# One order of work items per place in a group: four lists instead of one

## The chip, the cores and the metric

The kernel runs on one NeuronCore of one Trainium2 chip. The metric is device time in microseconds, the median of the runs shown. The engines are TensorE (PE, with its weight loads PEld), VectorE (DVE), ScalarE (ACT), GpSimd (POOL) and SyncE (SP, which here issues DMAs).

## The reference

Two branches of the same input x (2048 tokens, 640 wide) are mixed by a gate per token.

```python
def _A_ref(x, mem0, Wq, Wk, Wv, Wo, seg_len):      # 32 heads of 192, seg_len 32, M = 8 memory rows
    ...
    for s in range(n_seg):                          # 64 segments
        xs = x[:, s * seg_len:(s + 1) * seg_len, :].copy()
        h = jnp.concatenate([mem, xs], axis=1)      # 40 rows
        q, k, v = ...                               # h times Wq, Wk, Wv
        scores = jnp.einsum('bhqe,bhke->bhqk', q, k) * scale
        scores = jnp.where(mask[None, None], scores, -1000000000.0)
        p = _softmax(scores, axis=-1)
        o = jnp.einsum('bhqk,bhke->bhqe', p, v)
        o = jnp.einsum('bhte,hed->btd', o, Wo)
        mem = o[:, :M, :].copy()                    # memory of the next segment
        outs.append(o[:, M:, :])
    ...
g = _sigmoid((x * gate_w).sum(-1, keepdims=True))
return g * a + (1 - g) * b                          # b: a gated GELU feed-forward of x
```

The eight memory rows of a segment come out of the segment before it, so the 64 segments form a chain.

## The kernel before

The feed-forward branch and the gate come first (about 177 us). Then `segment(s)` is called for s = 0 to 63. Four segments form a group; a segment's place in its group is q = s % 4.

The rows that go through the chain are 32: the 8 memory rows and the first 24 rows of the segment's own. The other 8 own rows ("left" rows) do not feed the memory of their own segment; their Q, K and V are computed for four segments at once, in 32 rows, ahead of time.

The 32 heads are handled in four octets of eight heads. Even segments go through octets 0, 1, 2, 3, odd ones through 3, 2, 1, 0; i below counts in the order of use. `PROG` is the hand-written order of a segment's items, and the order of each engine's instructions follows from it. All engines work their own queue in that order, and SP issues its DMAs in that order too. The items:

- `("g", n, k)`: projections, contraction slice k of 5, of the matrices in `GROUPS[n]`. n = 0 is Q and K of octet 0; 1 is V 0, Q 1, K 1; 2 is V 1, Q 2; 3 is K 2; 4 is V 2, Q 3; 5 is K 3; 6 is V 3. Each matrix takes four 384-wide matmuls (L1039, or L226 where the loaded rows are kept). In place 0 the V of the left rows goes along from octet 1 on. After k = 4 ACT copies the results out of PSUM (L1059 for Q and K, L1062 for V).
- `tq`, `tk`: DVE transposes Q or K (L1073). `sc`: mask and scores on PE (L1080, L1088, L1093), then maximum and subtraction on DVE (L1107, L1109). `ex`: exponential on ACT (L1119), sum, reciprocal and two products on DVE (L1121 to L1126).
- `pt`: p is transposed on PE (L1139, L1144) and copied by ACT (L1157; for the last octet L1151 and DVE's L1153). `pv`: p times V on PE (L1172, L1174), copied into `uT` by ACT (L1183; a part of the last octet by DVE, L1188).
- `("wo", i, h)`: two pairs of heads of octet i times their rows of Wo, L1201 for octets 0 to 2, L1224 for the last. After `wo 2 1` ACT and DVE add the four partial sums (`half_sums`, L1207, L1210). In place 3 `wo` also multiplies the left rows (L1201 again).
- `("lf", q, u, k)`: in place q, Q and K of the left rows of a later group, unit u, slice k (L882 and L226). `("le", q, u, m)`: their copy (ACT, L887) and transpose (DVE, L889); for m = 1 also a store to HBM on SP's queue (L893). An `le` that stands behind the last `wo` is put off until Z and the transposed memory are done. `("vb", k)`: in place 3, V of the left rows for the next group (L1012). Items for another place are skipped.

At the end of a segment DVE adds up Z (L1340) and transposes the memory rows (L1344, `Tm`), and the next segment's first Q waits for that.

Most weights stay in SBUF. Seventeen pieces do not fit twice: octet 0's and octet 3's slices of Q, K and V (14 of 15) share slots, and three pieces of Wo share slots with three others. `swap_loads` is called after each item: a piece that has just been used is replaced by its partner (L597), which is wanted at the end of the same segment. So each segment loads 14 pieces of 384 KB and three of 480 KB, issued by SP in the order of use: K's slice 0, Q, K, V, Wo. Behind them in SP's queue stand the load of left Q and K for the next segment (`stg_load`, issued at `sc 3`, L942), the loads of the other branch's result (L947, L951), and the stores (L893, L951, L956).

PSUM banks for projections, `lf` and `pv` come from `misc_bank`, the least recently taken of those that are free in the list's order.

Of the kernel before, what the change touches and what calls it, by code (L numbers as in the profile page):

```python
# [231 lines left out]
def _build(nc, A_x, A_mem0, A_Wq, A_Wk, A_Wv, A_Wo, seg_len, w_gate, w_up, w_down,  # L232
# [9 lines left out]
    KT = Dm // 128  # L242
# [3 lines left out]
    NOCT = NT // 4  # L246
# [251 lines left out]
    def piece_view(key, o):  # L498
        if key[0] == 3:
# [1 line left out]
        return bview(o, GQ)  # L501

    GROUPS = [[(0, 0), (1, 0)], [(2, 0), (0, 1), (1, 1)], [(2, 1), (0, 2)], [(1, 2)], [(2, 2), (0, 3)], [(1, 3)], [(2, 3)]]
    PROG = [("g", 0, 0), ("g", 0, 1), ("g", 0, 2), ("g", 0, 3), ("g", 0, 4), ("g", 1, 0), ("g", 1, 1), ("tq", 0),
# [13 lines left out]
    assert NOCT == 4  # L518
    WOP = 4
    NWP = NT  # L520
# [4 lines left out]
    def octet(s, i):  # L525
        return i if s % 2 == 0 else NOCT - 1 - i
# [4 lines left out]

    def seg_order(s):
        keys = []
        for item in PROG:
            if item[0] == "g":
                keys += [(m, octet(s, i), item[2]) for m, i in GROUPS[item[1]]]
            elif item[0] == "wo":
                keys += [(3, p) for p in wo_pairs(s, item)]
        return keys

    orders = [seg_order(0), seg_order(1)]
    assert len(orders[0]) == len(set(orders[0])) == 3 * KT * NOCT + NWP
    partner = {}
    for m, k in [(m, k) for m in range(3) for k in range(KT)][3 * KT - NSQ:]:
# [53 lines left out]
               dma_sem="slot%d" % slot_id[key], name="%s %s" % (name, key))  # L598

    def piece(seg, key):  # L600
        order = orders[seg % 2]
        oi = last_req.get(seg, -1) + 1
        assert order[oi] == key, "pieces must be consumed in order"
        last_req[seg] = oi
        if seg == 0 and key in tmp_off:
            return left_piece(key)
        done_keys.append(key)
        return piece_view(key, res_off[key]), r_res[key]
# [15 lines left out]
    def left_piece(key):  # L624
        if key in tmp_off:
            return piece_view(key, tmp_off[key]), r_tmp[key]
        return piece_view(key, res_off[key]), r_res[key]
# [616 lines left out]
                                      pa == p_first and c == 0, pb == p_last and c == 2),  # L1244
                       reads=[ra, rb, r_uTl[pa // 4]], writes=[r_ps[LB]], name="Wol s%d p%d" % (s, pa))

    assert PROG.index(("g", [n for n, ms in enumerate(GROUPS) if (2, 1) in ms][0], KT - 1)) < PROG.index(("wo", 0, 0))
    late_at = ("g", 1, KT - 1)
    items = [item for item in PROG if item[0] not in ("lf", "le", "vb")]
    n_wo = PROG.index(items[-1])  # L1250
    rowl = [bview(wsB_off["rowl"], 768) for b in range(2)]
    r_rowl = [sreg(wsB_off["rowl"], 768) for b in range(2)]
    nqkv = [i for i, item in enumerate(PROG) if item[0] == "g"][-1]

    def left_evac(s, u, m):
        left_rows(*unit(s, u), m, lb[u, m], lst[3], r_lst[3], rowl[m], r_rowl[m])
# [7 lines left out]

    def segment(s):
        g, q = s // 4, s % 4
        held = []
        post = []
        for n, item in enumerate(PROG):
            kind, i = item[0], item[1]  # L1270
            if kind == "g":
                if n == 0:
                    left_fill(s, octet(s, 0))
                    if s:
                        S_.add("pool", lambda e: e.memset(pl_sb[0:104, :, M * ((q + 3) % 4):M * ((q + 3) % 4) + M], 0.0),
                               writes=[r_p], name="pl zero s%d" % s)
                proj(s, item)
                ki = [j for m, j in GROUPS[i] if m == 1 and item[2] == KT - 1]
                kind, i = ("k", ki[0]) if ki else ("", 0)
                if kind == "k" and i == 1:  # L1280
                    if s > 0:
                        out_store(s - 1)
                    if s + 1 < NSEG:
                        x_load(s + 1)
            elif kind == "tq":
                row_transp(s, 0, i)
            elif kind == "tk":
                row_transp(s, 1, i)
            elif kind == "sc":
                scores(s, i)  # L1290
                if i == 0 and q == 0 and g > 0:
                    left_sums(g - 1)
            elif kind == "ex":
                softmax(s, i)
            elif kind == "pt":
                p_transp(s, i)
            elif kind == "pv":
                pv_oct(s, i)
            elif kind == "lf":
                if i == q and unit(s, item[2]):  # L1300
                    if item[3] == 0:
                        for m in range(2):
                            lb[item[2], m] = misc_bank(s)
                    for m in range(2):
                        LBK[m] = lb[item[2], m]
                    left_mm(*unit(s, item[2]), item[3], unit_piece)
            elif kind == "vb":
                if q == 3 and g + 1 < NG:
                    if i == 0:
                        lb["v"] = misc_bank(s)  # L1310
                    vl_mm(s + 1, i)
            elif kind == "le":
                if i == q and unit(s, item[2]):
                    if n > n_wo:
                        post.append(item[2:])
                    else:
                        left_evac(s, *item[2:])
            else:
                held = wo_part(s, item)
                if i == 2 and item[2] == 0 and q == 0 and g > 0:  # L1320
                    outl_store(g - 1)
                if q == 3 and item != items[-1]:
                    wo_left(s, held)
            swap_loads(s, item)
            if s == 0 and item == ("g", 0, KT - 1):
# [114 lines left out]
```

## Time and profile before

| | |
|---|---|
| time, median of 3 runs | 1790.21 us (1785.28 to 1790.6) |
| span of the profiled execution, first to last instruction | 1783.4 us |
| mean granted TensorE clock | 0.998 |
| PE busy | 1629.5 us, 91% |
| DVE, ACT, POOL busy | 54%, 45%, 18% |
| moved by DMA | 524.33 MB, mean 294 GB/s |
| start of the first segment, of the last | 176.9 us, 1752.2 us |

For the profiled execution the page gives the span only; its own time is not listed apart from the three runs. A row of the timeline has the start, the length, the engine, the line, the operation, what it writes and reads with shapes, how many were merged, and in brackets the idle time before and who ended it. A row of the waits has the waiting engine and line, who was waited for, the sum in us, how often, and the longest.

### The profile page before, as it was taken

How to read it: one execution, taken by the hardware profiler on the slowest of the kernel's cores; microseconds unless marked ns; L12 is line 12 of the kernel's file. 1: busy time of each engine (PE TensorE's matmuls, PEld its weight loads, DVE VectorE, ACT ScalarE, POOL GpSimd, SP SyncE). 2: the span in 40 equal slices, each digit the busy share in tenths (PEclk: the TensorE clock that was granted, in tenths of full speed). 3: DMA queues.
4: the chain of work that ended last, by engine and by line, in shares of the span. 5: the costliest groups of instructions: out<-in, count | busy, mean ns of one | idle time of the engine just before them, and what ended most of it. 6: DMA issues, size and time to landing. Idle time of an engine off the chain costs nothing.

```text
span 1783.4 us, 80070 instructions
## 1 busy us (share of the span) xinstructions
PE 1629.5 (91%) x39162; PEld 817.9 (46%) x31501; DVE 957.7 (54%) x2932; ACT 793.8 (45%) x1835; POOL 319.8 (18%) x1099
## 2 busy tenths in 40 slices
PE   9999989899998999899899999899999989899987
PEld 4554444454444444454444444454444444454443
DVE  2223555555555655555565655555555655555554
ACT  3222444444444444444444444444444544444443
POOL 1100111111211111111111111111211111111211
PEclk9999999999999999999999999999999999999999
DMA  9815887888788887888788887888888887888786
GB/s 332 297 45 177 329 318 266 324 322 316 289 295 298 318 311 261 318 318 315 287 299 299 311 319 263 322 310 319 298 299 300 317 290 269 321 313 321 289 303 260
DMA packets 263390, 524.33 MB, mean 294 GB/s; under 512 B 97384, under 2 KB 116224, under 8 KB 263040
## 3 DMA queue, kind: packets, MB, share of 16 engines
q1 hardware_dynamic: 259912, 516.11, 79.5%
q8 instruction: 276, 4.52, 1.0%
q10 hardware_dynamic: 3128, 3.09, 0.5%
q14 instruction: 74, 0.61, 0.1%
HBM read 498.00 MB, written 21.11 MB: 291 GB/s over the span
## 4 chain that ended last, share of the span: by engine, by line
PE 69%; DMA 13%; DVE 8%; ACT 6%; issue 4%; SPq 0%; DVEq 0%; ACTq 0%
PE ps L1039 20%; PE ps L226 15%; PE ps L1201 8%; DMA arena<-in_A_Wv_dram 7%; PE ps L1172 3%; DMA left_qk_scratch<-arena 3%; PE ps L802 3%; PE ps L799 3%; PE ps L882 3%; DVE arena L889 3%; PE ps L1093 2%; PE ps L817 2%; ACT arena L887 2%; PE ps L1080 2%; PE ps L1088 2%
## 5 line engine op out<-in xcount | busy, mean ns | idle before, releaser
L1039 PE MATMUL ps<-arena 128*32 128x384 bf16 x9940 | 734.8, 328 | 58.5 <-DVE arena L1344 40.4
L226 PE MATMUL ps<-arena 128*32 128x384 bf16 x7680 | 584.4, 326 | 10.8 <-ACT arena L887 6.1
L1039 PEld LDWEIGHTS ps<-arena 128*32 128x32 bf16 x9940 | 254.0, 96 | 420.1 <-issue 244.4
L1073 DVE STREAM_TRANSPOSE arena<-arena 128x384 bf16<-128x384 bf16 x512 | 279.0, 564 | 227.0 <-ACT arena L1059 226.6
L1059 ACT ACTIVATE arena<-ps 128x384 bf16<-128x384 f32 x512 | 236.2, 489 | 176.3 <-PE ps L1039 164.4
L1201 PE MATMUL ps<-arena 128*32 128x320 bf16 x6144 | 297.0, 300 | 16.1 <-issue 15.5
L1201 PEld LDWEIGHTS ps<-arena 128*32 128x32 bf16 x6144 | 163.6, 97 | 75.7 <-issue 26.5
L1119 ACT ACTIVATE ps<-ps 104x160 f32<-104x160 f32 x256 | 74.3, 290 | 236.4 <-DVE ps L1109 236.4
L1107 DVE TENSOR_REDUCE arena<-ps 104x4 f32<-104x160 f32 x256 | 83.1, 325 | 176.0 <-PE ps L1093 175.7
L1157 ACT ACTIVATE arena<-ps 128x448 bf16<-128x448 f32 x192 | 104.8, 546 | 143.3 <-PE ps L1144 143.3
L1191 POOL COPY arena<-arena 128x96 bf16<-128x96 bf16 x256 | 68.4, 267 | 522.6 <-ACT arena L1183 419.3
L936 POOL COPY arena<-arena 128x96 bf16<-128x96 bf16 x256 | 70.0, 274 | 498.7 <-PE ps L1093 436.3
L1183 ACT ACTIVATE arena<-ps 128x480 bf16<-128x480 f32 (+1 forms) x256 | 138.1, 540 | 34.0 <-PE ps L1174 29.0
L1062 ACT ACTIVATE arena<-ps 128x384 bf16<-128x384 f32 x256 | 124.8, 488 | 52.7 <-PE ps L1039 52.4
L1172 PE MATMUL ps<-arena 128*64 128x160 bf16 x1536 | 122.1, 243 | 10.4 <-issue 3.4
L1172 PEld LDWEIGHTS ps<-arena 128*64 128x64 bf16 x1536 | 80.6, 109 | 97.9 <-ACT arena L1157 46.6
L882 PE MATMUL ps<-arena 128*32 128x384 bf16 x1280 | 111.1, 330 | 1.2 <-issue 1.2
L1174 PE MATMUL ps<-arena 128*64 128x64 bf16 x1536 | 105.1, 194 | 5.8 <-issue 5.8
L1121 DVE TENSOR_REDUCE arena<-ps 104x4 f32<-104x160 f32 x256 | 81.8, 320 | 51.6 <-ACT ps L1119 43.9
L889 DVE STREAM_TRANSPOSE arena<-arena 128x384 bf16<-128x384 bf16 x128 | 73.8, 577 | 57.4 <-ACT arena L887 52.6
L1224 PE MATMUL ps<-arena 128*32 128x160 bf16 x3072 | 77.1, 234 | 22.2 <-DMA arena<-in_A_Wo_dram 12.6
L887 ACT ACTIVATE arena<-ps 128x384 bf16<-128x384 f32 x128 | 62.4, 490 | 67.6 <-DVE arena L889 38.5
(84 smaller groups left out, 1816.7 us busy)
## 6 DMA issues: line engine op xcount, KB each, us to landing
arena<-in_A_Wk_dram SPq DMA_DIRECT2D x335, 384.0 KB, 7.7
arena<-in_A_Wv_dram SPq DMA_DIRECT2D x335, 384.0 KB, 9.4
arena<-in_A_Wq_dram SPq DMA_DIRECT2D x272, 384.0 KB, 5.6
arena<-in_A_Wo_dram SPq DMA_DIRECT2D x205, 480.0 KB, 7.4
left_qk_scratch<-arena SPq DMA_DIRECT2D x64, 192.0 KB, 2.6
arena<-left_qk_scratch SPq DMA_DIRECT2D x63, 192.0 KB, 7.8
ffn_b_scratch<-arena ACTq DMA_DIRECT2D x16, 160.0 KB, 3.7
arena<-ffn_b_scratch SPq DMA_DIRECT2D x64, 40.0 KB
```

The lines of the kernel that those rows point to most:

```text
L226: return e.add_instruction(mybir.InstMatmult(name=nm, start_tensor_calc=like["start"], stop_tensor_calc=stop, tile_size=(128, 32), tile_po ...
L882: fns.append(lambda e, outp=outp, rhs=rhs, j=j: e.matmul(outp, lhs, rhs, start=(k == 0), stop=(k == KT - 1), tile_position=(0, 32 * j)))
L889: S_.add("dve", lambda e: e.transpose(out=dst[:, :, m].rearrange("p q c i -> p c q i"), in_=rowl.rearrange("p (c r) -> p c r", r=L)), read ...
L1039: fns.append(lambda e, outp=outp, rhs=rhs, j=j: e.matmul(outp, lhs, rhs, start=(k == 0), stop=(k == KT - 1), tile_position=(0, 32 * j)))
L1059: S_.add("act", lambda e, m=m, bk=bk: e.activation(out=rows_sb[m], in_=ps[:, bk, 0:384], func=ACTF.Copy), reads=[r_ps[bk]], writes=[r_rows ...
L1062: S_.add("act", lambda e, i=i, bk=bk: e.activation(out=v_sb[i % NVB].rearrange("p (c n) -> p c n", c=3), in_=ps[:, bk, 0:384].rearrange("p ...
L1073: S_.add("dve", lambda e: e.transpose(out=dst[:, :, 0:L], in_=rows_sb[m].rearrange("p (c r) -> p c r", r=L)), reads=[r_rows[m]], writes=[r ...
L1157: S_.add("act", lambda e: e.activation(out=PT, in_=ps[:, bank, 0:PTW + 128], func=ACTF.Copy), reads=[r_ps[bank]], writes=[r_PT], name="pT ...
L1172: return [lambda e: e.matmul(full, v[:, e0:e0 + 64], PTm[:, i], start=True, stop=False, tile_position=(0, 64 * i), skip_group_check=True), ...
L1174: lambda e: e.matmul(part, vl[:, e0:e0 + 64], PTl[:, i], start=False, stop=True, tile_position=(0, 64 * i), skip_group_check=True)]
L1183: S_.add("act", lambda e: e.activation(out=apx(u[:, 0, 0, :], [[R, na], [3 * R, 4], [1, R]]), in_=ps[:, A, 0:na * W].rearrange("p (c t r) ...
L1201: fns.append(lambda e, i=i, t=t, j=j, gv=gv: e.matmul(ps[32 * j:32 * j + 32, bank, 0:2 * DJ].rearrange("p (h n) -> p h n", h=2), lhs2[i], ...
```

## The change

The single list `PROG` gives way to four lists, `PROGS[q]`, one for each place. Each holds the items that its place runs, and all are in a new order. What each item does is not touched. The bookkeeping follows: four orders of weight pieces instead of two, the last `wo` and the last `g` found in each list, and the start of a segment recognised by `("g", 0, 0)`, since the list of place 1 begins with an `lf`.

```diff
-    PROG = [("g", 0, 0), ("g", 0, 1), ("g", 0, 2), ("g", 0, 3), ("g", 0, 4), ("g", 1, 0), ("g", 1, 1), ("tq", 0),
-   ("tk", 0), ("g", 1, 2), ("sc", 0), ("ex", 0), ("g", 1, 3), ("g", 1, 4), ("tq", 1), ("g", 2, 0),
-   ("g", 2, 1), ("g", 2, 2), ("g", 2, 3), ("tk", 1), ("g", 2, 4), ("g", 3, 0), ("pt", 0), ("g", 3, 1),
-   ("sc", 1), ("tq", 2), ("lf", 1, 0, 0), ("ex", 1), ("g", 3, 2), ("g", 3, 3), ("g", 3, 4), ("lf", 1, 0, 1),
-   ("pv", 0), ("g", 4, 0), ("tk", 2), ("g", 4, 1), ("g", 4, 2), ("g", 4, 3), ("pt", 1), ("sc", 2),
-   ("lf", 1, 0, 2), ("g", 4, 4), ("pv", 1), ("g", 5, 0), ("tq", 3), ("ex", 2), ("lf", 1, 0, 3), ("g", 5, 1),
-   ("lf", 1, 0, 4), ("g", 5, 2), ("wo", 0, 0), ("le", 1, 0, 0), ("le", 1, 0, 1), ("g", 5, 3), ("wo", 0, 1),
-   ("lf", 1, 1, 0), ("lf", 0, 1, 0), ("pt", 2), ("wo", 1, 0), ("g", 5, 4), ("pv", 2), ("wo", 1, 1), ("tk", 3),
-   ("sc", 3), ("lf", 0, 1, 1), ("g", 6, 0), ("lf", 1, 1, 1), ("g", 6, 1), ("lf", 2, 1, 0), ("g", 6, 2),
-   ("ex", 3), ("g", 6, 3), ("wo", 2, 0), ("lf", 2, 1, 1), ("lf", 1, 1, 2), ("pt", 3), ("g", 6, 4),
-   ("wo", 2, 1), ("lf", 2, 1, 2), ("pv", 3), ("lf", 2, 1, 3), ("lf", 0, 1, 2), ("vb", 0), ("lf", 1, 1, 3),
-   ("vb", 1), ("lf", 1, 1, 4), ("lf", 0, 1, 3), ("lf", 0, 1, 4), ("lf", 2, 1, 4), ("vb", 2), ("le", 0, 1, 0),
-   ("le", 1, 1, 0), ("le", 1, 1, 1), ("le", 2, 1, 0), ("wo", 3, 0), ("le", 2, 1, 1), ("wo", 3, 1), ("vb", 3),
-   ("le", 0, 1, 1), ("vb", 4)]
+    PROGS = [
+        [("g", 0, 0), ("g", 0, 1), ("g", 0, 2), ("g", 0, 3), ("g", 0, 4), ("g", 1, 0), ("g", 1, 1), ("g", 1, 2),
+   ("tq", 0), ("tk", 0), ("sc", 0), ("g", 1, 3), ("ex", 0), ("g", 1, 4), ("tq", 1), ("g", 2, 0), ("tk", 1),
+   ("g", 2, 1), ("g", 2, 2), ("g", 2, 3), ("pt", 0), ("g", 2, 4), ("g", 3, 0), ("sc", 1), ("g", 3, 1),
+   ("g", 3, 2), ("g", 3, 3), ("tq", 2), ("pv", 0), ("ex", 1), ("g", 3, 4), ("g", 4, 0), ("tk", 2), ("g", 4, 1),
+   ("g", 4, 2), ("g", 4, 3), ("g", 4, 4), ("g", 5, 0), ("lf", 0, 1, 0), ("g", 5, 1), ("lf", 0, 1, 1),
+   ("sc", 2), ("g", 5, 2), ("pt", 1), ("g", 5, 3), ("tq", 3), ("lf", 0, 1, 2), ("wo", 0, 0), ("lf", 0, 1, 3),
+   ("g", 5, 4), ("tk", 3), ("ex", 2), ("lf", 0, 1, 4), ("pv", 1), ("g", 6, 0), ("g", 6, 1), ("le", 0, 1, 0),
+   ("g", 6, 2), ("pt", 2), ("sc", 3), ("g", 6, 3), ("wo", 0, 1), ("le", 0, 1, 1), ("ex", 3), ("pv", 2),
+   ("g", 6, 4), ("wo", 1, 0), ("pt", 3), ("wo", 1, 1), ("wo", 2, 0), ("pv", 3), ("wo", 2, 1), ("wo", 3, 0),
+   ("wo", 3, 1)],
+        [("lf", 1, 0, 0), ("g", 0, 0), ("g", 0, 1), ("g", 0, 2), ("g", 0, 3), ("g", 0, 4), ("lf", 1, 0, 1),
+   ("g", 1, 0), ("tk", 0), ("tq", 0), ("g", 1, 1), ("g", 1, 2), ("g", 1, 3), ("g", 1, 4), ("sc", 0),
+   ("g", 2, 0), ("lf", 1, 0, 2), ("g", 2, 1), ("tk", 1), ("ex", 0), ("g", 2, 2), ("tq", 1), ("g", 2, 3),
+   ("g", 2, 4), ("g", 3, 0), ("lf", 1, 0, 3), ("lf", 1, 0, 4), ("g", 3, 1), ("sc", 1), ("pt", 0), ("g", 3, 2),
+   ("g", 3, 3), ("g", 3, 4), ("tk", 2), ("pv", 0), ("g", 4, 0), ("g", 4, 1), ("g", 4, 2), ("tq", 2),
+   ("g", 4, 3), ("ex", 1), ("sc", 2), ("g", 4, 4), ("g", 5, 0), ("g", 5, 1), ("g", 5, 2), ("le", 1, 0, 0),
+   ("g", 5, 3), ("tq", 3), ("pt", 1), ("g", 5, 4), ("ex", 2), ("tk", 3), ("pv", 1), ("g", 6, 0),
+   ("le", 1, 0, 1), ("wo", 0, 0), ("wo", 0, 1), ("g", 6, 1), ("lf", 1, 1, 0), ("pt", 2), ("lf", 1, 1, 1),
+   ("sc", 3), ("ex", 3), ("lf", 1, 1, 2), ("pv", 2), ("lf", 1, 1, 3), ("wo", 1, 0), ("lf", 1, 1, 4),
+   ("le", 1, 1, 0), ("pt", 3), ("g", 6, 2), ("g", 6, 3), ("g", 6, 4), ("le", 1, 1, 1), ("wo", 1, 1),
+   ("wo", 2, 0), ("pv", 3), ("wo", 2, 1), ("wo", 3, 0), ("wo", 3, 1)],
+        [("g", 0, 0), ("g", 0, 1), ("g", 0, 2), ("g", 0, 3), ("g", 0, 4), ("g", 1, 0), ("tq", 0), ("g", 1, 1),
+   ("g", 1, 2), ("tk", 0), ("g", 1, 3), ("g", 1, 4), ("sc", 0), ("lf", 2, 1, 0), ("g", 2, 0), ("g", 2, 1),
+   ("g", 2, 2), ("lf", 2, 1, 1), ("tq", 1), ("g", 2, 3), ("tk", 1), ("ex", 0), ("g", 2, 4), ("sc", 1),
+   ("g", 3, 0), ("g", 3, 1), ("g", 3, 2), ("g", 3, 3), ("lf", 2, 1, 2), ("pt", 0), ("g", 3, 4), ("ex", 1),
+   ("lf", 2, 1, 3), ("pv", 0), ("g", 4, 0), ("g", 4, 1), ("lf", 2, 1, 4), ("g", 4, 2), ("g", 4, 3), ("tk", 2),
+   ("tq", 2), ("g", 4, 4), ("pt", 1), ("g", 5, 0), ("sc", 2), ("g", 5, 1), ("wo", 0, 0), ("ex", 2),
+   ("g", 5, 2), ("g", 5, 3), ("g", 5, 4), ("g", 6, 0), ("pv", 1), ("pt", 2), ("g", 6, 1), ("tq", 3), ("tk", 3),
+   ("wo", 0, 1), ("pv", 2), ("sc", 3), ("le", 2, 1, 0), ("ex", 3), ("le", 2, 1, 1), ("wo", 1, 0), ("wo", 1, 1),
+   ("g", 6, 2), ("wo", 2, 0), ("g", 6, 3), ("pt", 3), ("g", 6, 4), ("pv", 3), ("wo", 2, 1), ("wo", 3, 0),
+   ("wo", 3, 1)],
+        [("g", 0, 0), ("g", 0, 1), ("g", 0, 2), ("g", 0, 3), ("g", 0, 4), ("g", 1, 0), ("g", 1, 1), ("tq", 0),
+   ("tk", 0), ("g", 1, 2), ("sc", 0), ("g", 1, 3), ("ex", 0), ("g", 1, 4), ("g", 2, 0), ("g", 2, 1), ("tq", 1),
+   ("tk", 1), ("g", 2, 2), ("g", 2, 3), ("pt", 0), ("g", 2, 4), ("g", 3, 0), ("g", 3, 1), ("pv", 0), ("sc", 1),
+   ("tq", 2), ("g", 3, 2), ("g", 3, 3), ("g", 3, 4), ("g", 4, 0), ("wo", 0, 0), ("g", 4, 1), ("g", 4, 2),
+   ("tk", 2), ("ex", 1), ("sc", 2), ("pt", 1), ("g", 4, 3), ("g", 4, 4), ("wo", 0, 1), ("g", 5, 0),
+   ("g", 5, 1), ("ex", 2), ("g", 5, 2), ("pv", 1), ("g", 5, 3), ("g", 5, 4), ("tk", 3), ("g", 6, 0), ("tq", 3),
+   ("pt", 2), ("g", 6, 1), ("wo", 1, 0), ("g", 6, 2), ("pv", 2), ("sc", 3), ("ex", 3), ("g", 6, 3), ("vb", 0),
+   ("wo", 1, 1), ("pt", 3), ("g", 6, 4), ("wo", 2, 0), ("pv", 3), ("vb", 1), ("wo", 2, 1), ("wo", 3, 0),
+   ("wo", 3, 1), ("vb", 2), ("vb", 3), ("vb", 4)]]
...
-        for item in PROG:
+        for item in PROGS[s % 4]:
-    orders = [seg_order(0), seg_order(1)]
+    orders = [seg_order(s) for s in range(4)]
...
-        order = orders[seg % 2]
+        order = orders[seg % 4]
...
-    assert PROG.index(("g", [n for n, ms in enumerate(GROUPS) if (2, 1) in ms][0], KT - 1)) < PROG.index(("wo", 0, 0))
+    for prog in PROGS:
+        assert prog.index(("g", [n for n, ms in enumerate(GROUPS) if (2, 1) in ms][0], KT - 1)) < prog.index(("wo", 0, 0))
-    items = [item for item in PROG if item[0] not in ("lf", "le", "vb")]
-    n_wo = PROG.index(items[-1])
+    last_wo = ("wo", NOCT - 1, 1)
+    n_wos = [prog.index(last_wo) for prog in PROGS]
-    nqkv = [i for i, item in enumerate(PROG) if item[0] == "g"][-1]
+    nqkvs = [max(i for i, item in enumerate(prog) if item[0] == "g") for prog in PROGS]
...
+        n_wo, nqkv = n_wos[q], nqkvs[q]
-        for n, item in enumerate(PROG):
+        for n, item in enumerate(PROGS[q]):
-                if n == 0:
+                if item[1:] == (0, 0):
...
-                if q == 3 and item != items[-1]:
+                if q == 3 and item != last_wo:
```

## The prediction

> **What bounds the kernel now.** I read the page first, then the engine's waits for PE, then the same stretch of four segments in windows, then the timeline around each wait.
>
> ```profile
> PE 1629.5 (91%) x39162; PEld 817.9 (46%) x31501; DVE 957.7 (54%) x2932; ACT 793.8 (45%) x1835; POOL 319.8 (18%) x1099
> ...
> q1 hardware_dynamic: 259912, 516.11, 79.5%
> q8 instruction: 276, 4.52, 1.0%
> ```
>
> PE is the busy engine, but the weight queue q1 is close behind it. The windows of one group, places 0 to 3 (segments 36 to 39), show how little room each place has:
>
> ```profile
> 1079.78:1105.13 25.35, 23.59 (x615) 12.05 (x492) 15.51 (x49) 11.97 (x29) 5.42 (x18) 1.00 0.79 292
> 1105.13:1131.07 25.94, 23.42 (x593) 10.67 (x454) 15.19 (x47) 12.65 (x30) 4.55 (x16) 1.00 0.83 301
> 1131.07:1154.61 23.54, 21.25 (x553) 9.99 (x433) 13.63 (x44) 11.39 (x27) 4.49 (x16) 1.00 0.88 323
> 1154.61:1180.10 25.49, 23.66 (x628) 12.81 (x528) 12.60 (x42) 10.79 (x26) 4.49 (x16) 1.00 0.80 297
> ```
>
> Columns: length, busy PE, PEld, DVE, ACT, POOL, clock, DMA share, GB/s. Over all 16 groups the places take 25.13, 25.74, 23.91 and 25.35 us, together 100.1. Place 2 has least PE work and the busiest transfers. What PE waits for:
>
> ```profile
> PE ps L1039 <- DVE arena L1344: 40.4, 48, 1.8
> PE ps L1201 <- issue: 15.5, 23, 1.7
> PE ps L1224 <- DMA arena<-in_A_Wo_dram: 12.6, 22, 0.9
> PE ps L1039 <- DMA arena<-in_A_Wv_dram: 9.3, 19, 1.6
> PE ps L1139 <- DVE arena L1125: 7.8, 22, 0.7
> ```
>
> The first is the segment boundary (last `wo`, Z, transpose Tm, next Q): from the last 160-wide matmul group to the next Q 0.95 us pass instead of 0.07. Two are weights that have not landed. Place 2 on PE:
>
> ```profile
> 1147.75 0.34 PE L1039 MATMUL ps<-arena 128*32 128x384 bf16 x4
> 1148.49 0.35 PE L1039 MATMUL ps<-arena 128*32 128x384 bf16 x4 [0.41 <-DMA arena<-in_A_Wv_dram]
> ...
> 1152.00 0.81 PE L1224 MATMUL ps<-arena 128*32 128x160 bf16 x36
> 1153.25 0.39 PE L1224 MATMUL ps<-arena 128*32 128x160 bf16 x12 [0.44 <-DMA arena<-in_A_Wo_dram]
> 1154.61 0.35 PE L1039 MATMUL ps<-arena 128*32 128x384 bf16 x4 [0.97 <-DVE arena L1344]
> 1154.78 0.34 PE L226 MATMUL ps<-arena 128*32 128x384 bf16 x4
> ```
>
> The trace's landings explain it (means of segments 8 to 55, from the segment's first Q): in places 0, 2 and 3 the first swapped piece is issued at 0.54 and lands at 4.2 to 4.4, then one lands every 1.0 to 1.4 us: last K at 13.4, V at 14.4, 15.5, 16.5, 17.5 and 18.7, the three Wo at 19.9, 21.2 and 22.4. No order of items makes them earlier. The last Wo then needs its matmuls and the boundary, some 1.35 us, so 23.8 us is a floor for a place; place 2 stands on it. Place 1 runs 1.1 us late from the start, because a store of left rows waits at the head of SP's queue:
>
> ```profile
> 1106.33 0.38 SPq L893 DMA_DIRECT2D left_qk_scratch<-arena  x1
> ...
> 1106.76 0.50 SPq L597 DMA_DIRECT2D arena<-in_A_Wk_dram  x1
> ```
>
> Place 1 began at 1105.13: its first swap goes out at 1.63 there. On average its first lands at 5.6, its last V at 20.2, its last Wo (behind a second store) at 24.4.
>
> **The method.** I price each item by the distance between starts on PE: four 384-wide matmuls 0.163 us (1154.61 to 1154.78 above), a `wo` 0.405 (0.41 for the last octet), `sc` 0.6, `pt` 0.1, `pv` 0.52. Both orders hold the same items in each place, so the sums are the same, 22.06, 21.24, 19.61 and 22.04 us, 85.0 in all. The other 15.1 us of a group are waits. I walk each new list at these prices and compare the PE work between producer and user with the time that the trace shows for the step: last K matmul start to Tk's end 1.5 (1.9 for a Q and K pair); `sc` to the probabilities p 2.5 to 2.6 (max 0.33, subtract 0.33, exp 0.29, sum 0.32, reciprocal 0.18, p 0.39, with hand-overs); `pt` to its copy 0.9; V's last matmul to its copy 0.9; `pv` to uT's copy 1.1.
>
> **Place 1, the gain.** `le 0 1 1` moves from behind the last `wo` of place 0 into its list, so the store is issued inside place 0 and place 1's stream starts at 0.54, not 1.62. `lf 1 0 0` (0.33 us) now stands ahead of place 1's first Q and runs inside the boundary wait. The second store still stands before the Wo loads: V's last at 18.7 and 4.2 us from there as in place 1 now (20.2 to 24.4) give the last Wo at 22.9. Waits that remain: `pv 0` (0.49 us of work behind `pt 0`, 0.25 short), a last K piece 0.2, `pv 1` 0.45, uT before the last `wo` 0.5, boundary 1.0. They end at the same point as the transfers: 24.25, so -1.5 us.
>
> **Place 0, a loss.** `ex 2` stands behind `g 5 4` and `tk 3`. From K's last matmul its copy (0.87), the transpose, then sum, reciprocal and p take 2.4 us; only 1.75 lie before `pt 2`: 0.54 short after other delays (now 0.15). The second bank of `lf 0 1 1` is released 0.14 late. `sc 1` loses 0.1, `pt 3` 0.1 (two left transposes of 0.58 stand among the softmax's DVE steps), `wo 3 0` 0.26 (only `wo 2 1` between `pv 3` and it), the boundary 0.2, since the two partial sums of 0.32 now follow `wo 2 1` late. The waits before `pv 2` and `pv 3` go (-0.4). Sum +0.8 net of rounding.
>
> **Place 2, even.** Gone: the wait before `pt 2` 0.56, late V and K pieces 0.7, late Wo 0.54, boundary 0.2. New: `pv 0` 0.25, `sc 2` 0.15, the first two V pieces 0.3 (the list wants them at 13.5 and 14.3), `pt 3` 0.7 (1.54 us behind `sc 3`, a left transpose between), `pv 3` 0.9: it stands directly behind `g 6 4`, and V's copy follows the copy of `pt 3` on ACT. Sum +0.15 after a shorter wait before `wo 3 0`.
>
> **Place 3, a loss.** The list wants V's first two pieces at 13.6 and 13.9; with 0.65 of earlier delays they are wanted at 14.3 and 14.8 and land at 14.5 and 15.5: 0.25 and 0.75. `pt 3` has 1.14 us behind `sc 3`, now 1.46: 0.94 instead of 0.44. `pv 0` 0.2. Gone: 0.35 before `wo 3 0`, 0.3 of smaller waits, 0.1 at the boundary, where `vb 2` to `vb 4` now cover. The V wait also swallows some 0.55 of the 1.4 us "issue" idle that this place has now (the part that falls ahead of it). Sum +0.4.
>
> **Instruction fetch.** The rows "PE <- issue" add up to 36.5 us, 2.3 a group, and each long one ends about 2.45 us after an instruction packet started (276 packets, 16.4 KB each). The new lists put more of the short `wo` matmuls side by side. Counting the stretches of 120 instructions that PE runs through in less than 2.45 us, their shortfall grows from 2.97 to 3.45, a sixth: +0.3 a group, between -0.3 and +1.0 as single packets fall. [...]
>
> **Sum.** +0.8 -1.5 +0.15 +0.4 +0.3 = +0.15 us a group; 0.1 a place for waits that such a walk misses makes +0.55, and 16 groups +9. The profiled span of 1783.4 becomes 1792; the runs' median stands 6.8 above the span, which stays, so 1799. Nothing changes ahead of 177 us, in the feed-forward part. DVE's and ACT's work is the same, and a wait on SP costs what is queued behind it: the only such shift is the store, priced above.
>
> **Rivals.** (a) Faster: place 1 gains its 1.5 us and the chains behind `sc 3` are covered, since a late V piece and the late p overlap on PE instead of adding up. Then place 0 loses 0.3, place 3 and fetch nothing, place 2 gains 0.15: -1.35 a group, 1768. For it: V waits sit between `sc 3` and `pt 3` in place 2 now and `pt 3` waits only 0.08 there. Against: in the new lists the V waits come before `sc 3`. It decides at `pt 3` of place 3. (b) Clearly slower: place 1's gain halves, because the store moved into place 0 and the early `stg` load delay the third Wo there and the next stream's first landing (4.2 now, 4.4 and more behind stores), and fetch takes 1.0: +2.0 a group, 1822. (c) No change: +-0.3 a group. That the change does nothing is out: the lists differ in every place.
>
> **Chances.** Forecast 0.42, (a) 0.34, (b) 0.14, (c) 0.10. A measurement of this kernel tells about 0.3% (5.4 us). The forecast's own range is 1793 to 1810, of which a little lies within 0.3%. So faster 0.37, same 0.12, slower 0.51. The range for eight in ten reaches to (a) and most of the way to (b): 1768 to 1818.
>
> **What would show it.** Right: place 1 near 24.3 us with its first swap issued at 0.5; V waits at `g 6 0` and `g 6 1` in place 3; longer idle before L1139 (pT) and before L1172 of place 2; place 0 longer by half a microsecond or more. Wrong: idle before L1139 no longer than now, or place 1's stream still starting behind a store.

## The result, and the profile after

The changed kernel took 1809.59 us (median of 7 runs, 1803.16 to 1812.88), the kernel before 1790.60 us on the same chip (7 runs, 1785.28 to 1799.40): ratio 1.0098 [1.0076, 1.0119]. That is slower, as forecast, but by 19 us where the forecast had 9.

The two profiled executions lie at the far ends of their sets (spans 1783.4 and 1811.1 us), so they differ by 27.7 us, more than the medians do. Most lines of the code have moved by 27: projections are now L1066, `wo` L1228 (last octet L1251), `pt` L1166, `pv` L1199, the left store L920, left copy and transpose L914 and L916, swaps L624, Tm L1373, V's copy L1089, the second copy of the last pT L1180. `stg_load` is L932 in the kernel before (not L942, which loads the other branch's result) and L959 now.

The page shows the same work and the same bytes, with the clock lower (a mean of 0.985 where before had 0.998):

```profile
PE 1631.2 (90%) x39181; PEld 810.1 (45%) x31501; DVE 943.3 (52%) x2932; ACT 793.6 (44%) x1835; POOL 319.6 (18%) x1099
```

The windows of segments 36 to 39, places 0 to 3 (columns as in the prediction):

```profile
1098.93:1124.56 25.63, 24.06 (x629) 11.46 (x497) 15.76 (x50) 12.17 (x29) 5.25 (x18) 1.00 0.86 297
1124.56:1151.17 26.61, 22.30 (x585) 10.60 (x450) 14.41 (x46) 12.24 (x29) 4.72 (x17) 1.00 0.83 293
1151.17:1176.49 25.32, 22.33 (x553) 10.42 (x433) 13.16 (x44) 11.68 (x27) 4.49 (x16) 0.93 0.84 300
1176.49:1201.33 24.84, 22.80 (x630) 12.48 (x531) 12.61 (x42) 10.55 (x26) 4.48 (x16) 1.00 0.80 296
```

Place 1, which was to gain most, is the longest, and place 2 shows a clock of 0.93. Over groups 2 to 15 (counted from 1, so without the first and the last) the places take 25.48, 25.91, 25.30 and 25.44 us. The prediction's 25.13, 25.74, 23.91 and 25.35 us are of these 14 groups as well, not of all 16. So the places change by +0.35, +0.17, +1.39 and +0.09, in sum +2.0 us a group. These are of one execution of each kernel; the seven runs of the changed kernel spread over 10 us, 0.6 us a group, so a place that moves by 0.1 or 0.2 us says little. PE's waits:

```profile
PE ps L1066 <- DVE arena L1373: 35.2, 48, 1.1
PE ps L1251 <- DMA arena<-in_A_Wo_dram: 34.0, 35, 2.2
PE ps L1066 <- DMA arena<-in_A_Wv_dram: 19.2, 46, 1.0
PE ps L1166 <- DVE arena L1152: 17.5, 29, 1.0
PE ps L1066 <- DMA arena<-in_A_Wk_dram: 10.2, 22, 0.7
PE ps L1199 <- ACT arena L1089: 9.3, 16, 0.6
```

The boundary wait is about what it was (40.4 before). The wait for Wo has grown from 12.6 to 34.0 us, V from 9.3 to 19.2, p (L1152, 7.8 before) to 17.5, and the wait for V's copy ahead of `pv 3` is all but new. The rows "PE <- issue" fell from 36.5 to 15.4 us in sum.

The Wo wait sits at the end of place 1. PE's timeline across the boundary of segments 25 and 26:

```profile
838.57 0.39 PE L1251 MATMUL ps<-arena 128*32 128x160 bf16 x12 [0.54 <-DMA arena<-in_A_Wo_dram]
840.73 0.39 PE L1251 MATMUL ps<-arena 128*32 128x160 bf16 x12 [1.78 <-DMA arena<-in_A_Wo_dram]
841.76 0.51 PE L1066 MATMUL ps<-arena 128*32 128x384 bf16 x4 [0.64 <-DVE arena L1373]
842.06 0.54 PE L226 MATMUL ps<-arena 128*32 128x384 bf16 x4
842.38 0.54 PE L1066 MATMUL ps<-arena 128*32 128x384 bf16 x4
...
844.99 0.50 PE L226 MATMUL ps<-arena 128*32 128x384 bf16 x8
```

Two waits and the boundary leave PE almost empty, and then place 2's first groups of four matmuls start 0.32 us apart, not 0.16, until 844.7. Windows around it show why:

```profile
837.88:841.29 3.41, 0.93 (x30) 0.38 (x24) 0.75 (x3) 0.20 (x1) 0.26 (x2) 1.00 0.89 278
841.29:844.70 3.41, 2.94 (x40) 0.84 (x24) 1.08 (x5) 0.00 (x0) 1.17 (x4) 0.50 0.32 65
844.70:848.11 3.41, 3.41 (x94) 1.09 (x46) 1.19 (x3) 1.81 (x5) 0.12 (x1) 1.00 1.02 346
```

After a stretch of 3.41 us in which PE was busy for 0.93 us, the granted clock is 0.50 for the next 3.41 us. The trace has 12 such halved stretches of 3.41 or 6.83 us inside the chain of segments, 9 of them at the end of place 1 or the start of place 2. The profiled run of before has one.

Why Wo is late: SP's queue in segment 37 (place 1, start 1124.56).

```profile
1125.10 0.35 SPq L624 DMA_DIRECT2D arena<-in_A_Wk_dram  x1
...
1141.21 0.38 SPq L920 DMA_DIRECT2D left_qk_scratch<-arena  x1
1141.63 2.29 SPq L624 DMA_DIRECT2D arena<-in_A_Wo_dram  x3
```

The first swap goes out at 0.54, as forecast. Then the store of `le 1 0 1` (the prediction's second store) waits at the head of the queue until 16.65, and all three Wo are issued behind it. The transfers in 1140 to 1152, as the DMA view gives them (GB/s in 40 equal slices of 0.3 us; below, KB each and median us from issue to landing):

```profile
GB/s 393 376 348 237 209 78 72 255 305 96 29 12 102 77 141 282 384 435 423 397 435 410 410 410 384 464 254 310 330 298 287 120 117 56 35 20 3 0 0 0
...
arena<-in_A_Wo_dram SPq DMA_DIRECT2D x3, 480.0 KB, 4.6
```

By the time the Wo are issued the queue has all but run dry. Only the tail of V's last piece is left, which lands at 18.54, and the store; in the ten slices from 1141.5 on 117 GB/s are moved on average, then the stream starts anew. On average (segments 8 to 55) place 1's Wo are issued at 17.11, 18.01 and 18.53 and land at 21.47, 22.98 and 24.72.

### The profile page after: what moved, and what is told of

Read it like the earlier page. It is cut to its first block, busy times and chain, and to the rows that moved or that the text cites. A ratio compares the mean times of both kernels' runs of the same rounds, so it can differ in the third digit from the quotient of the medians.

```text
span 1811.1 us, 80133 instructions
## 1 busy us (share of the span) xinstructions
PE 1631.2 (90%) x39181; PEld 810.1 (45%) x31501; DVE 943.3 (52%) x2932; ACT 793.6 (44%) x1835; POOL 319.6 (18%) x1099
## 5 line engine op out<-in xcount | busy, mean ns | idle before, releaser
L1066 PE MATMUL ps<-arena 128*32 128x384 bf16 x9940 | 747.7, 332 | 72.5 <-DVE arena L1373 35.2
L226 PE MATMUL ps<-arena 128*32 128x384 bf16 x7680 | 592.6, 332 | 7.1 <-DVE arena L1237 3.5
L1066 PEld LDWEIGHTS ps<-arena 128*32 128x32 bf16 x9940 | 255.6, 97 | 453.2 <-issue 263.2
L1100 DVE STREAM_TRANSPOSE arena<-arena 128x384 bf16<-128x384 bf16 x512 | 273.1, 559 | 174.0 <-ACT arena L1086 173.5
L1086 ACT ACTIVATE arena<-ps 128x384 bf16<-128x384 f32 x512 | 236.8, 490 | 282.4 <-PE ps L1066 266.0
L1228 PE MATMUL ps<-arena 128*32 128x320 bf16 x6144 | 295.3, 301 | 8.9 <-issue 6.2
L1228 PEld LDWEIGHTS ps<-arena 128*32 128x32 bf16 x6144 | 166.0, 97 | 95.3 <-issue 23.6
L1089 ACT ACTIVATE arena<-ps 128x384 bf16<-128x384 f32 x256 | 125.0, 488 | 160.9 <-PE ps L1066 159.6
L1184 ACT ACTIVATE arena<-ps 128x448 bf16<-128x448 f32 x192 | 104.5, 544 | 114.9 <-PE ps L1171 114.4
L1199 PE MATMUL ps<-arena 128*64 128x160 bf16 x1536 | 118.7, 243 | 19.1 <-ACT arena L1089 9.3
L1199 PEld LDWEIGHTS ps<-arena 128*64 128x64 bf16 x1536 | 79.9, 109 | 98.4 <-ACT arena L1184 38.9
L1251 PE MATMUL ps<-arena 128*32 128x160 bf16 x3072 | 83.0, 237 | 34.4 <-DMA arena<-in_A_Wo_dram 34.0
L909 PE MATMUL ps<-arena 128*32 128x384 bf16 x1280 | 109.0, 327 | 0.0
L916 DVE STREAM_TRANSPOSE arena<-arena 128x384 bf16<-128x384 bf16 x128 | 72.8, 569 | 32.9 <-ACT arena L914 28.6
L1136 DVE TENSOR_TENSOR ps<-ps,arena 104x160 f32<-104x160 f32 x256 | 85.0, 332 | 8.8
```

Source lines behind the costliest of these rows:

```text
L226: return e.add_instruction(mybir.InstMatmult(name=nm, start_tensor_calc=like["start"], stop_tensor_calc=stop, tile_size=(128, 32), tile_po ...
L909: fns.append(lambda e, outp=outp, rhs=rhs, j=j: e.matmul(outp, lhs, rhs, start=(k == 0), stop=(k == KT - 1), tile_position=(0, 32 * j)))
L1066: fns.append(lambda e, outp=outp, rhs=rhs, j=j: e.matmul(outp, lhs, rhs, start=(k == 0), stop=(k == KT - 1), tile_position=(0, 32 * j)))
L1086: S_.add("act", lambda e, m=m, bk=bk: e.activation(out=rows_sb[m], in_=ps[:, bk, 0:384], func=ACTF.Copy), reads=[r_ps[bk]], writes=[r_rows ...
L1089: S_.add("act", lambda e, i=i, bk=bk: e.activation(out=v_sb[i % NVB].rearrange("p (c n) -> p c n", c=3), in_=ps[:, bk, 0:384].rearrange("p ...
L1100: S_.add("dve", lambda e: e.transpose(out=dst[:, :, 0:L], in_=rows_sb[m].rearrange("p (c r) -> p c r", r=L)), reads=[r_rows[m]], writes=[r ...
```

## The experiments

Theory A: place 1's late Wo, behind the store, are the main loss, and the halved clock is their consequence. Rivals: B, the halved clock is a loss of its own that covering the gap removes; C, places 2 and 3 (the chains behind `sc 3`) carry the loss; D, instruction fetch does. Every ratio is against the kernel before on the same chip; what a place takes is the mean of groups 2 to 15 of the profiled execution. "Old list" is a place's part of `PROG` in the kernel before. The median of the kernel before itself lay between 1790 and 1798 us in these comparisons, so ratios are compared, not times.

**e1: the store behind two Wo.** In place 1's new list:

```diff
-   ("le", 1, 0, 1), ("wo", 0, 0), ("wo", 0, 1), ("g", 6, 1),
+   ("wo", 0, 0), ("wo", 0, 1), ("le", 1, 0, 1), ("g", 6, 1),
```

> The changed kernel with one swap in place 1: le 1 0 1, with its store on SP's queue, stands behind wo 0 0 and wo 0 1 instead of ahead of them. Theory A (the late last Wo of place 1, held up behind the store, costs the time, partly through the half-clock stretches that follow the idle PE): the Wo loads are issued near 14.7 us of place 1 instead of 17.1 to 18.5, the last lands near 22.5 instead of 24.7, place 1 goes from 25.9 to about 24.2 us, most of the twelve half-clock stretches go, and the time falls from 1810 to 1770 to 1785. Rival B (the longer chains behind sc 3 in places 0, 2 and 3 cost the time, and place 1 is bound by them just as well): the wait for Wo turns into another one, place 1 stays above 25.3 and the time stays at 1803 to 1812.

Measured 1850.62 us, 1.0307 [1.0264, 1.0351], place 1 at 28.56. On the transfers theory A held: with the store behind them, the Wo are issued at 15.43 to 16.38, the last lands at 22.70 instead of 24.72, and the Wo wait goes (34.0 to 2.5 us). But the waits show another in its place, DVE's first, then PE's:

```profile
DVE arena L916 <- DMA left_qk_scratch<-arena: 64.9, 15, 6.2
```

```profile
PE ps L1228 <- DVE arena L1180: 52.8, 15, 5.1
...
PE ps L1251 <- DMA arena<-in_A_Wo_dram: 2.5, 7, 0.8
```

The left rows have one staging buffer (`lst[3]`): the next left transpose (L916) waits until the store has landed, which is now queued behind 1.4 MB of Wo. Behind that transpose on DVE stands the copy of the last pT, and PE waits for it. So the store can't go behind the loads.

**e5: the store on ACT's queue**, issued behind `sc 3`, so that it stands ahead of no Wo load on SP:

```diff
-        if m:
+        if m and s % 4 == 1 and u == 0:
+            on_act.append(unit(s, u))
+        elif m:
...
+                if i == 3 and on_act:
+                    left_store(*on_act.pop(), 3, eng="act")
```

> The changed kernel with the first store of left rows in place 1 issued from ACT's queue, behind sc 3, instead of from SP's; nothing else moves. In e1 the store behind the Wo loads landed late and the next left transpose, which writes the same staging rows, held up DVE. Here the store no longer stands ahead of the Wo loads nor behind them. Theory A (the Wo loads of place 1 come late only because they stand behind that store on SP): Wo is issued at 14.5 to 15.5 us of place 1, the last lands near 22.5 instead of 24.7, the store lands near 20 as now, place 1 falls from 25.9 to 24.2 to 24.6, the half-clock stretches at the start of place 2 go, clock above 0.993, and the time is 1775 to 1790. Rival B (place 1 is bound elsewhere as well): place 1 stays above 25.3 and the time above 1803.

Measured 1850.83 us, 1.033 [1.0302, 1.0359], place 1 again at 28.56. The Wo land at 20.1, 21.6 and 23.3, some 1.4 us earlier, but the store lands so late that the next transpose starts at 23.67:

```profile
DVE arena L916 <- DMA left_qk_scratch<-arena: 63.0, 15, 5.5
```

**e8: a mix**: e5's store, place 2's old list, and `wo 0 1` moved up in place 0 (behind `lf 0 1 3`).

> The changed kernel with what the runs so far speak for: place 0's new list with wo 0 1 moved up ahead of g 5 4 (its Wo swap issued near 16 instead of 19.4 us), place 1's new list with the store on ACT's queue, place 2's list of before, place 3's new list. Theory A: places of about 24.9, 24.3, 23.8 and 25.3 us, 98.3 a group against 100.1 before: 1760 to 1775, faster than both. Rival (each wait that goes turns into another): 1785 to 1800.

Measured 1849.49 us, 1.0319 [1.0294, 1.0345], place 1 at 28.97: e5's wait stays and settles the time. The other two parts can be read in their own places. Place 2 takes 24.49 where e5 has 25.05. In place 0 the third Wo is issued at 16.20 instead of 19.51, lands at 22.75, and PE no longer waits for it; still the place takes 25.64 where e5 has 25.50, since waits for p and "issue" come in its stead.

**e9: the store earlier.** If it can go neither behind the loads nor late, it has to be ready before they are wanted:

```diff
-   ("sc", 2), ("g", 4, 4), ("g", 5, 0), ("g", 5, 1), ("g", 5, 2), ("le", 1, 0, 0),
+   ("sc", 2), ("le", 1, 0, 0), ("le", 1, 0, 1), ("g", 4, 4), ("g", 5, 0), ("g", 5, 1), ("g", 5, 2),
...
-   ("le", 1, 0, 1), ("wo", 0, 0), ("wo", 0, 1), ("g", 6, 1),
+   ("wo", 0, 0), ("wo", 0, 1), ("g", 6, 1),
```

> The changed kernel with le 1 0 0 and le 1 0 1 of place 1 moved up, right behind sc 2. The store is then issued near 14 us of place 1, ahead of the Wo loads but no longer holding them up, and lands behind the last V piece near 19.3, before the next left transpose needs the staging rows. Theory A (place 1 is late because this store stands at the head of SP's queue when the Wo loads should go out): Wo is issued at 15 to 16 instead of 17.1 to 18.5, the last lands at 22.9 to 23.2 instead of 24.7, DVE isn't held up as in e1 and e5, place 1 falls from 25.9 to 24.4 to 24.9, half-clock stretches at the start of place 2 become few, time 1783 to 1795. Rival B (with Wo in time another wait takes its place): place 1 stays above 25.3 and the time at 1803 to 1812.

Measured 1791.95 us against 1798.29 for the kernel before: 0.9965 [0.9948, 0.9982]. The store goes out at 14.27 and lands at 19.37; the Wo are issued at 16.08 to 17.10 and land at 20.48, 21.95 and 23.53. Places: 25.28, 24.96, 24.71, 25.25. PE's waits, and places 1 and 2 of the same group in windows:

```profile
PE ps L1199 <- ACT arena L1184: 24.8, 61, 1.5
...
PE ps L1251 <- DMA arena<-in_A_Wo_dram: 8.4, 14, 1.6
```

```profile
1101.76:1126.40 24.64, 21.81 (x584) 10.81 (x449) 14.48 (x46) 12.25 (x29) 4.51 (x17) 1.00 0.89 316
1126.40:1150.35 23.95, 20.96 (x554) 10.16 (x434) 13.22 (x44) 11.58 (x27) 4.53 (x17) 1.00 0.86 317
```

Place 1 is 1.97 us shorter than after's in this group and moves 316 GB/s instead of 293; the halved stretches in the chain fall from 12 to 2. Two items at another point of one list turn the change from 1% slower to 0.35% faster: theory A. Over all groups place 1 gives 0.95 us of this and place 2, with one halved segment instead of eight, 0.59. The edit moves the copies and transposes of these left rows along with the store, and no run has the store's place alone. A new wait shows in place 1 (`pv` for the copy of pT, L1184, 24.8 us in all), and it is cheaper: 1.20 us a segment there, 0.28 in after, while the Wo wait goes from 1.74 to 0.28.

**e2: PE kept busy in the gap**, for theory B. Six 512-wide matmuls whose result nobody reads stand between the last two `wo` of place 1:

```diff
+                if q == 1 and item == ("wo", NOCT - 1, 0):
+                    fb = misc_bank(s)
+                    S_.add("pe", [... 6 matmuls of 512 columns ...], writes=[r_ps[fb]], ...)
```

> The changed kernel with six matmuls of 512 columns, which nobody reads, added on PE between wo 3 0 and wo 3 1 of place 1, where PE now waits for Wo; six of them take about 1.3 us. Theory A2 (the half-clock stretches come from too little PE work in the 3.4 us before them): they disappear from the start of place 2, the granted clock rises from 0.985 towards 0.995, and the time falls by 5 to 15 us although PE does more. Rival (the stretches have another cause, or cost nothing because PE waits for transfers anyway): clock as it was and time unchanged or up to 10 us longer.

Measured 1811.65 us, 1.0103 [1.0065, 1.0142]: no gain. The clock did recover, as the view of the cores shows (after, then e2):

```profile
core 0: 1811.1 us, clock 0.985
```

```profile
core 0: 1811.0 us, clock 0.996
```

Place 2 is 0.6 us shorter (24.70) and has 3 halved segments of 14 where after has 8. But place 0 lost 0.3 us, all of it "issue" (0.11 to 0.55), and in the whole trace "PE <- issue" rose from 15.4 to 29.5 us. So the halved clock costs about 0.6 us a group in place 2 (e9 gives the same there), and the filler paid for it in "issue" waits: all 27 of those of more than 0.5 us end 2.2 to 2.6 us after an instruction packet started.

**e3 and e4: which list.** e3 is after with place 1's old list. e4 is before with one item moved, so that place 1's stream starts early in the old order:

```diff
-   ("le", 1, 1, 0), ("le", 1, 1, 1), ("le", 2, 1, 0), ("wo", 3, 0), ("le", 2, 1, 1), ("wo", 3, 1), ("vb", 3),
-   ("le", 0, 1, 1), ("vb", 4)]
+   ("le", 0, 1, 1), ("le", 1, 1, 0), ("le", 1, 1, 1), ("le", 2, 1, 0), ("wo", 3, 0), ("le", 2, 1, 1),
+   ("wo", 3, 1), ("vb", 3), ("vb", 4)]
```

> The changed kernel with place 1's list put back to the items and order of before; the other three lists are new. Theory A: place 1 keeps the early start of its stream (the store is issued inside place 0), its Wo loads are issued in time, its last Wo lands near 23.2, place 1 takes 24.5 to 24.9 us instead of 25.9, and the time falls to 1785 to 1795. Rival B: place 1's list isn't what costs; the time stays at 1803 to 1812.

> The kernel before with one item of place 0 moved: le 0 1 1, with its store, stands ahead of wo 3 0 instead of behind the last wo. Theory A (the store at the head of SP's queue delays place 1's whole stream of weights by 1.1 us): place 1's first swap is issued at 0.5 instead of 1.6 us, its last Wo lands near 23.2 instead of 24.4, place 1 falls from 25.7 to 24.5, and the time from 1790 to 1770 to 1776. Rival: place 1 is bound by PE's waits and the transfers only follow; 1785 to 1792.

e3 measured 1801.51 us, 1.0042 [1.0016, 1.0067]: about 10 us come back where 15 to 25 were expected. The last Wo of place 1 lands at 23.25, as expected, and the Wo waits are down to 5.6 us in the whole trace. But place 1 takes 25.59, with waits of 1.42 at the boundary behind it (0.66 in after) and 0.6 for the left rows' copy on ACT (L914). e4 measured 1802.14 us, 1.004 [1.002, 1.006], where a gain was expected: place 0 lost 1.1 us (its left copy and transposes now stand ahead of Z), and place 1 gained 0.23 only, though its last Wo lands at 23.30, as expected. The boundary wait tells why:

```profile
PE ps L1039 <- DVE arena L1344: 64.2, 48, 2.0
```

It was 40.4 us before. Behind place 0 it is now 1.76 us a segment (0.67 before), behind place 1 1.40 (0.89 before). With an early stream the end of place 1 in the old order is set by its left rows: both matrices use the same `rowl` buffer, so the second copy waits for the first transpose, and Z's adds stand behind the second transpose on DVE. In e4 they start 0.84 us after the last `wo` of place 1 has ended, 0.37 us in the kernel before. So the transfers were not all that held place 1 in the old order, where the prediction spoke of its late stream alone.

**e6 and e7: after with place 2's old list, and with place 0's.**

> The changed kernel with place 2's list put back to the order of before. Theory A, second part (pv 3 directly behind g 6 4 and pt 3 behind sc 3 cost place 2 about 1.0 us beside the clock): place 2 goes from 25.3 to 24.1 to 24.4 (the half-clock stretches that place 1 leaves behind stay), 16 to 20 us less, 1790 to 1795. Rival (place 2 is bound by its transfers, 23.8 us and more, whatever the list): 1803 to 1812.

> The changed kernel with place 0's list put back to the order of before, so that the store of le 0 1 1 again stands at the head of SP's queue when place 1 begins. Theory A: place 0 falls from 25.5 to about 25.2, but place 1's stream starts 1.1 us later, its K pieces and its last Wo come later still, and place 1 grows from 25.9 to 26.5 to 27.5: 1815 to 1830. Rival (place 0's new list is a loss by itself and place 1 doesn't feel the store): 1800 to 1806.

e6 measured 1798.78 us, 1.0044 [1.0017, 1.0072]: about 10 us of the 19 come back where 16 to 20 were expected; place 2 takes 24.57. So theory C holds for place 2, in part. The old list of place 2 is worth 0.73 us there in e6, 0.56 in e8 against e5, and 0.63 in e10 against e9. e7 measured 1828.12 us, 1.0193 [1.0157, 1.0229]: with `le 0 1 1` back behind the last `wo`, place 1's stream is late again and it takes 27.42 instead of 25.91. The swapped pieces of K show it (10.2 us in after):

```profile
PE ps L1066 <- DMA arena<-in_A_Wk_dram: 32.3, 50, 2.2
```

**e10 and e11: the better parts together.** e10 is e9 with place 2's old list, e11 is e10 with place 3's old list too.

> e9 with place 2's list of before. Theory A, both parts: the two gains add up, 1770 to 1783, faster than the kernel before. Rival (only one of the two counts, since they share the transfers): 1788 to 1798.

> e10 with place 3's list of before as well, so that only places 0 and 1 are new. My walk had place 3's new list 0.4 us longer; the trace of the changed kernel shows it 0.1 us longer with half-clock stretches and 0.1 shorter without. If the walk is right, 6 us less than e10; if the trace is, within 3 us of e10.

e10 measured 1782.98 us, 0.9928 [0.9903, 0.9953], and its profile has no halved stretch in the chain: faster than both kernels. The two gains nearly add up (1.33% in e9 and 0.54% in e6 off the ratio, 1.70% in e10). e11 measured 1786.61 us, 0.9933 [0.991, 0.9957]: place 3's new order is worth nothing that can be told, either way, and the 6 us that the walk promised don't show.

## Why the prediction was right in direction and short in size

The waits below are what the distance between two starts on PE has over the price of the item, as the prediction counted them (segments 8 to 55); the idle times in the rows are 0.2 to 0.3 us less each.

**Place 1: the step that failed.** Forecast -1.5, measured +0.17. The first half of its reasoning held: the first swap goes out at 0.54, K and V land as in the other places (V's last at 18.72, forecast 18.7), and e7, without the early store, is longer there by 27.42 - 25.91 = 1.5 us. What failed is "V's last at 18.7 and 4.2 us from there". In the kernel before two of the three Wo were issued ahead of the store and stood queued behind V. In the new list all three stand behind it, and the queue is nearly empty when they come: issue to landing takes 4.4 us for the first, and the last lands at 24.72 instead of 22.9. It shows as two Wo waits of 0.64 and 1.50 us on average, more than the 1.67 us between forecast and measurement. e1 shows the landing (22.70 with the store behind the Wo), and e9 what it costs: with the store earlier place 1 takes 24.96, 0.95 us less. That is still 0.71 over the forecast of 24.25; there the last Wo lands at 23.53, and `pv` waits 1.20 us for the copy of pT, so this rest isn't the store's alone.

**Place 2: mis-sized.** Forecast +0.15, measured +1.39; 0.96 in the segments without a halved clock. The named waits are there. PE's timeline at the end of segment 38:

```profile
1171.56 0.22 PE L1166 MATMUL ps<-arena 104*32 104x80 bf16 x4 [0.41 <-DVE arena L1152]
...
1172.32 0.34 PE L1066 MATMUL ps<-arena 128*32 128x384 bf16 x1 [0.26 <-DVE arena L1180]
1173.23 0.26 PE L1199 MATMUL ps<-arena 128*64 128x160 bf16 x2 [0.58 <-ACT arena L1089]
```

`pt 3` waits 0.57 on average (forecast 0.7). `pv 3` was priced at 0.9 and has an excess of 1.35, since the last `g` before it is held up as well, by the copy of pT (L1180), which was not in the sum. e6 gives this list's price over the old one with the rest as in after: 0.54% (1.0098 against 1.0044), some 10 us. Place 2 has the largest part of the measured loss, and some of that is the halved clock that place 1's waits set off.

**Halved clock: not in the sum at all.** Segments that it touches are longer than their like by 0.8 (place 1), 1.1 (place 2) and 0.9 us (place 3); spread over the groups that is at most 1.1 us a group, since a segment with a long wait is longer whatever the clock. e2, which removes most of them and little else in place 2, gives 0.6 there. Before's profiled run, from which every price was taken, had next to none of it (0.998), so its rows could not show what longer waits would set off. Its other runs beside the experiments stood at 0.991 to 1.0, those of after at 0.985 to 0.990.

**Place 0: over-sized.** Forecast +0.8, measured +0.35. `pt 2` waits about 0.33 where 0.54 was forecast, and a wait not forecast came in: the third Wo lands at 24.13, and PE waits 0.65 for it. Rival (b) named this wait, but for another reason: the Wo isn't held up by the store or by the `stg` load. `wo 0 1`, which frees its slot, stands late in the new list, so the load goes out at 19.42 in segment 36 and the store behind it at 19.79. Moving `wo 0 1` up removes the wait and not the time (e8).

**Place 3.** Forecast +0.4, measured +0.09. The V waits are 0.59 and 0.65 (forecast 0.25 and 0.75), `pt 3` waits 0.93 (forecast 0.94). What was over is other idle, which shrank: "issue" here fell from 1.37 to 0.86 us a segment.

**Instruction fetch: sign wrong.** Forecast +0.3 a group; "PE <- issue" fell by 21.1 us in all, 1.3 a group. A likely reason is that PE now waits for other things while the packets come; no run tests it. The stretch of 120 instructions that it counts with was the author's estimate; no run shows that figure. What the traces show is how often and where PE waits: 30 waits of more than 0.5 us for 276 packets before, 13 after, and the instructions that they hold up stand whole multiples of 256 apart on PE in each of these two traces, to within one (matmuls and weight loads counted together). With the shorter ones they sum to time that counts, 36.5 us before, 15.4 after and 29.5 us in e2.

**The rivals.** (a) fell where it was to be decided, at `pt 3` of place 3. (b) had the sum of +2.0 a group, but not the cause: fetch cost less, not more, the next stream's first landing was not delayed (4.0), the third Wo of place 0 came late for another reason, and place 1 lost to its own store.

**The sum.** +0.35 +0.17 +1.39 +0.09 = +2.0 a group against +0.55. Of the 1.45 between, place 1 is +1.67 and place 2 +1.24; places 0 and 3, the fetch and the margin take off 1.46. Times 16 this is 32 us; the spans differ by 27.7, the medians by 19, as the profiled run of before was its fastest and that of after its slowest. The prediction carried before's span-to-median distance of 6.8 us over, which was such an accident: in every run here the time is 1.7 to 2.0 us above its own span.

**How much was luck.** The direction came out right, but the forecast loss lay in places 0 and 3 and the fetch, and the measured one lies mostly in place 2, with place 1's gain gone. With about half of that gain in (24.96 against 25.74 before) and one halved segment instead of eight in place 2, lists that differ by two items are 0.35% faster than the kernel before (e9). So "slower" was right in part because an error that the prediction didn't see outweighed those that it made the other way.

## What to carry to other kernels

The 4.2 us between the landings of place 1's last V and its last Wo did not carry over to the new order, where they became 6.0 (18.72 to 24.72): look at what stands ahead of each load in its queue before and after, and at whether transfers are still running when it is issued. The store did best here where its data were ready early (e9, ratio 0.9965, against 1.0098 for the change alone); behind the loads it held the buffer that it reads, and the transposes of e1 waited 64.9 us for it. When a new order lengthens one wait, look at how empty TensorE's time around it becomes: here a stretch of 3.41 us with 0.93 us of busy PE was followed by 3.41 us at a granted clock of 0.50, in which groups of four matmuls started 0.32 us apart instead of 0.16.

## What the runs showed of the hardware that was not expected

- **Halved clock after a half-empty window.** All the halved stretches of after start on one grid of 3413.3 ns, to within 1 ns over 1577 us. All 8 grid windows in the chain with PE busy below 0.50 were followed by one, 4 of the 10 with 0.50 to 0.60, and none of the busier that ran at full clock. No sharp limit shows in these spans: in e4 six windows with 0.46 to 0.49 were followed by none. The clocks granted in the traces of before and after are 0.50 and 1.00, none between. The longest idle of PE ahead of each of the 12 stretches was 0.58 to 2.21 us, so several waits in one window, each shorter than the grid's step, were enough here.
- **First landings out of a drained queue.** In after the loads that went out when little was queued landed 3.4 to 4.4 us later: 3.4 to 3.6 us for the first 384 KB piece of a place (issued at 0.54 to 0.62), 4.4 for the first 480 KB Wo of place 1 (17.11 to 21.47). Behind others the 384 KB pieces landed 1.0 to 1.5 us apart, most of them. So place 1's first Wo, issued late, cost its whole way of 4.4 us, not only its share of the stream.
- **More "issue" idle with six more matmuls.** With six more matmuls and their weight loads in place 1 of each group (e2) it was 29.5 us instead of 15.4, and the increase fell in places 0 and 3. The count alone does not set it: the kernel before, with no more matmuls than after, had 36.5. The long waits end 2.2 to 2.6 us after an instruction packet started, in the kernel before, in after and in e2. The fetch traffic hardly differs (276 packets before and after the change, 277 in e2), so it seems a matter of where the packets fall; which rule places them was not settled.
